# Attention and feed-forward on one core: the global units' probabilities turned on VectorE, one start flag per bank, single transfers for the last chunk

## The chip, the cores and the metric

The kernel runs on one core of a Trainium2 chip. The metric is the time of one execution in microseconds (us) on the device. The kernel before took 938.16 us in the median of three runs (934.59 to 939.67). An engine has its own instruction stream and runs it in order; engines wait for each other by semaphores. PE is TensorE's matmul, PEld its weight load, DVE VectorE, ACT ScalarE, POOL GpSimd, SP the engine that issues all transfers.

## The reference, cut to what matters

There are 8 batches, 8 heads of 64 columns, 32 global and 512 local tokens per batch. Global tokens attend to everything, local tokens to the global ones and to a window of 32 to each side. The result goes through a layer norm and a two-layer feed-forward with a residual.

```
k_all, v_all = cat(k_g, k_l), cat(v_g, v_l)
out_g = softmax(scale * q_g @ k_all.T) @ v_all                  # 32 rows per batch and head, 544 keys
s_ll  = where(|i - j| <= 32, scale * q_l @ k_l.T, -1e9)
out_l = softmax(cat(scale * q_l @ k_g.T, s_ll)) @ v_all         # 512 rows per batch and head
x     = cat(out_g, out_l)  as [batch, 576, 512]
xn    = (x - mean) / sqrt(var + 1e-6) * g_ln
out   = x + relu(xn @ w_ch1) @ w_ch2                            # 512 -> 2048 -> 512
```

## The kernel before, in words

**Feed-forward.** The 4096 local tokens are cut into eight chunks of 512 (chunk 0 to 7), the 256 global ones are the last chunk, chunk 8. A chunk runs over 16 slices `f` of the hidden layer. Each slice has 12 matmuls `ph` (L739, `hidden`), a relu `hh` on ACT (L750), the rounding rest `hl` on DVE (L754), and for each of its four token tiles 3 matmuls `acc` (L766, `out`). The matmuls of `out` for slice `f-1` stand behind `hidden` of slice `f`, so that `hl` has time. Every operand is split into a high and a low part, hence the factor 3.

**Attention beside it.** While TensorE works on chunk c, the attention of the next chunk is fed in between, in small steps. `step()` is called seven times in a slice (before each third of `hidden`, and before each of the four `out`); each call takes one `yield` from a queue `first`, or else one from the queue `side`. `put(place, run)` hangs a piece of attention on a place of the chunk; place `2f` is before `hidden(f)`, place `2f+1` behind it. The order on every engine is the order in which the program writes it.

A *pair* is two head pairs of a half batch: scores on PE (`sc`, L428), the row minimum and mask on DVE (L446), exponentials on ACT, 16 steps of two 32x32-block transposes on DVE (`pt`, L490), values on PE (`pv`, L500), and a scaled output on DVE (`x`, L519). A chunk has four pairs, at the places 1, 9, 17 and 25.

A *global unit* is one head pair of the global tokens of four batches. There are eight (two batch groups, four head pairs); chunks 1 to 6 hold one each, chunk 7 two. Its scores come in two passes of 272 keys (`sc`, L566), each read from its two PSUM banks by two DVE instructions (`gp`, L576). Then exponentials on ACT (L589), eight 128x128 transposes on PE into PSUM (`t`, L607), copied to SBUF on ACT (`gpt`, L609), the last 32 keys by DVE (L608). The values are 40 matmuls into one bank (`pv`, L620), two heads one after the other; the trace counts each twice. DVE scales them (`gx`, L634), SP stores them to a buffer `xs` in DRAM in four transfers (L642) and loads the next unit's inputs (`gq`, `gk`, `gv`, `gvt`).

**PSUM.** Scores, transposes and global values share a pool of two banks (tag `att`), `ph` and the pairs' `pv` share another pool of two. A matmul that wants a bank waits until its last reader is done.

**End of a chunk.** At slice 14 SP loads the residual rows `ob` from `xs` (L784); at the end DVE adds `acc` (L799) and SP stores the rows (L801). In chunk 8 a token tile's rows come from four batches, and `rows_global` cuts each tile into four transfers of 32 rows:

```
def rows_global(bg):
    return [(slice(i * SG, (i + 1) * SG), (bg * BG + i) * SA, SG) for i in range(BG)]
...
host(globals_[c - 1], (5, 12, 15, 21))     # chunks 1..6: scores 0, scores 1, transposes, values
host(globals_[c - 1], (1, 4, 8, 12))       # chunk 7, first unit
host(globals_[c], (16, 18, 21, 23))        # chunk 7, second unit
```

**Start.** GpSimd builds a band and from it four mask tiles in 22 copies (L153, L155) before the first scores are reduced.

Of the kernel before, what the change touches and what calls it, by code (L numbers as in the profile page):

```python
# [11 lines left out]
F32 = mybir.dt.float32  # L12
# [9 lines left out]
P = 128  # L22
WIN = 32
# [61 lines left out]
def attention_ffn_kernel(  # L85
# [59 lines left out]
    masks = {}  # L145
    for half in range(2):
        for qb in range(2):
            m = const.tile([P, P], F32, name=f"mask{half}{qb}")
            nc.gpsimd.memset(m, 0.0)
            for g in range(4):  # L150
                gp = slice(g * WIN, (g + 1) * WIN)
                at = 3 - (4 * qb + g) % 3
                nc.gpsimd.tensor_copy(m[gp, :at * WIN], band[gp, g * WIN:(g + at) * WIN])  # L153
                if at < 3:
                    nc.gpsimd.tensor_copy(  # L155
                        m[gp, (at + 1) * WIN:], band[gp, (g + at) * WIN:(g + 3) * WIN]
                    )
            if half == qb == 0:
                nc.gpsimd.memset(m[:WIN, :WIN], NEG / QSCALE)
# [113 lines left out]
    class Local:  # L273
# [105 lines left out]
        def output(self):  # L379
            hp = self.at[1]  # L380
            x = token_tile(0, hp)
# [13 lines left out]
    class Pair:  # L395
# [118 lines left out]
        def output(self):  # L514
            hp = self.at[1]
            x = token_tile(self.chunk, hp)
            nc.vector.reciprocal(self.ri, self.ri)
# [11 lines left out]
        def store(self):  # L529
            store_x(self.at[0], self.at[2], ready[self.chunk][-1])  # L530

        def norm(self):
            x = ready[self.chunk][-1]
            xn = ready[self.chunk][-1] = new_x()
            return Norm(x, range(2), xn)

    class Global:


        def __init__(self, bg, hp):  # L540
            self.at = bg, hp
            self.next = None

        def load(self):
# [11 lines left out]
        def scores(self, part):  # L556
# [31 lines left out]
            for h in range(2):  # L588
# [8 lines left out]
                yield  # L597

        def transposes(self):
            p = self.p  # L600
            pt = apool.tile([P, 2, SA], F32, name="gpt", tag="gk")
            self.pt = pt[:, :, :4 * P].rearrange("p h (c q) -> p h c q", c=4)
            self.tail = pt[:, :, 4 * P:]
            for h in range(2):
# [7 lines left out]
        def values(self):  # L612
            bg, hp = self.at
            pv = ps_a.tile([P, 512], F32, name="pv", tag="att")
            for h in range(2):
                hd = slice(h * D, (h + 1) * D)
                for c in range(5):
                    for i in range(BG):
                        ip = slice(i * SG, (i + 1) * SG)
                        nc.tensor.matmul(  # L620
                            pv[ip, hd],
                            self.pt[:, h, c, ip] if c < 4 else self.tail[ip, h, :],
                            self.v[c // 2][:, i, c % 2, hd] if c < 4 else self.vt[ip, hd],
                            start=(c == 0),
                            stop=(c == 4),
                            tile_position=(0 if c < 4 else i * SG, i * SG),
                            skip_group_check=True,
                        )
            ri = small.tile([P, 2], F32, name="gri", tag="ri2")
# [9 lines left out]
            )  # L639
            for i in range(BG):  # L640
                r0 = (bg * BG + i) * SA
                nc.sync.dma_start(  # L642
                    xs[r0:r0 + SG, hp * P:(hp + 1) * P], x[i * SG:(i + 1) * SG, :]
                )
            if self.next:
# [3 lines left out]
    def load_global_tokens(bg):  # L649
        x = ready[last_chunk][0]  # L650
        for i in range(BG):
            r0 = (bg * BG + i) * SA
            nc.sync.dma_start(x[i * SG:(i + 1) * SG, bg, :], xs[r0:r0 + SG, :])
        yield

    def rows_local(b, t):
        r0 = b * SA + SG + t * P
        return [(slice(0, P), r0, P)]

    def rows_global(bg):  # L660
        return [(slice(i * SG, (i + 1) * SG), (bg * BG + i) * SA, SG) for i in range(BG)]

# [55 lines left out]
    class Ffn:  # L718
# [52 lines left out]
        def run(self, f0, rows, stage, next_chunk):  # L771
            nt = self.nt
            obs = []
            for f in range(f0, NF):
# [4 lines left out]
                side.append(stage(f, 1))  # L779
                if f == NF - 2:  # L780
                    ob = fpool.tile([P, 4, DM], F32, name="ob", tag="ob")
                    for t in range(nt):
                        for ps, r0, nr in rows[t]:
                            nc.sync.dma_start(ob[ps, t, :], xs[r0:r0 + nr, :])  # L784
                        obs.append(ob[:, t, :])
# [8 lines left out]
            for t in range(nt):  # L794
# [4 lines left out]
                nc.vector.tensor_tensor(obs[t], self.acc[t], obs[t], op=ALU.add)  # L799
                for ps, r0, nr in rows[t]:  # L800
                    nc.sync.dma_start(out_flat[r0:r0 + nr, :], obs[t][ps])  # L801

# [27 lines left out]
    weights = [Weights(f) for f in range(NF)]  # L830
    ready = {}
    turned = []

    def token_tile(c, hp):
        got = ready.setdefault(c, [])
        if hp == 0:
            got.append(new_x())
        return got[-1]

    wcm, wtmp = open_pool("wtmp")  # L840
    acm, apool = open_pool("apool")

    def attend(u, before):

# [25 lines left out]
        while True:  # L870
# [7 lines left out]
            n += 1  # L878
            yield
        for _ in more:  # L880
            pass
# [5 lines left out]
    class First:  # L887
# [11 lines left out]
        def norm(self, h):  # L899
            x = ready[0][h]  # L900
            self.norms.append(Norm(x, range(2), new_x()))
            self.norms[h].stats()
# [15 lines left out]
        def does(self, token):  # L918
# [22 lines left out]
            elif op == "Nx":  # L941
                store_x(*chunks[0][n[0]], ready[0][n[0]])
            elif op == "Qx":
# [37 lines left out]
    for c, chunk in enumerate(chunks):  # L981
        if c == 1:
            globals_[0].load()
        if chunk is None:
            rows = [rows_global(bg) for bg in range(NBG)]
        else:
            rows = [rows_local(b, 2 * half + j) for b, half in chunk for j in range(2)]
# [10 lines left out]
        if 0 < c < last_chunk - 1:  # L998
            for f in PAIR_STEPS:
                u, before = new.pop(0)  # L1000
                put(2 * f + 1, lambda u=u, before=before: attend(u, before))
# [114 lines left out]
```

## Time and profile before

| | us |
|---|---|
| three runs, median | 938.16 (934.59 to 939.67) |
| profiled execution, its time | 938.44 |
| profiled execution, its span in the trace | 936.7 |
| PE busy | 911.1 (97%) |
| DVE busy | 572.0 (61%) |
| ACT busy | 313.4 (33%) |
| POOL busy | 36.2 (4%) |

The span is what the trace covers; the profiled execution took 1.7 us more. PE's busy time counts pipelined matmuls whose modelled ends overlap the next starts, so what a matmul costs is read from starts or from the chain of waits. That chain is followed back from the last instruction, at each step to what released it. The granted TensorE clock was 1.00 (2.4 GHz) in every window from 209 us on.

### The profile page before, as it was taken

What the parts mean: (1) busy time and instruction counts of PE and PEld (TensorE: products, weight loads), DVE (VectorE), ACT (ScalarE), POOL (GpSimd) and SP (SyncE); (2) the same over time, 40 slices, a digit from 0 to 9 for tenths busy, and PEclk for the clock granted to TensorE, in tenths of its full rate; (3) what the DMA queues carried; (4) which work ended last, traced back from release to release, by engine and by line L of the source; (5) the groups of instructions that cost most, each with busy time, mean ns of one, the idle gap of its engine ahead of it and who ended that gap; (6) DMA issues with size and microseconds to landing.
All of it is one profiled execution on the core that took longest, in us unless ns stands there. A gap on an engine that the chain in (4) does not pass through costs nothing.

```text
span 936.7 us, 21033 instructions
## 1 busy us (share of the span) xinstructions
PE 911.1 (97%) x8652; PEld 722.4 (77%) x8652; DVE 572.0 (61%) x1852; ACT 313.4 (33%) x839; POOL 36.2 (4%) x121
## 2 busy tenths in 40 slices
PE   5899999999999999999999999999999999999997
PEld 3677777777778778777878778777877777777896
DVE  4999958765786657765776657765776623111311
ACT  5888733331323323231323323231422312211210
POOL 3000000000000000000000000000000000000000
PEclk9799999999999999999999999999999999999999
DMA  9993245212633263212533263213533151031100
GB/s 349 419 415 118 87 136 194 101 58 89 228 121 98 76 214 117 84 51 103 214 121 97 76 233 99 89 53 119 190 121 98 46 170 57 1 102 60 51 18 23
DMA packets 48880, 119.33 MB, mean 127 GB/s; under 512 B 5008, under 2 KB 16272, under 8 KB 45712
## 3 DMA queue, kind: packets, MB, share of 16 engines
q1 hardware_dynamic: 48784, 117.98, 35.4%
q8 instruction: 68, 1.11, 0.5%
q14 instruction: 28, 0.23, 0.1%
HBM read 100.14 MB, written 17.83 MB: 126 GB/s over the span
## 4 chain that ended last, share of the span: by engine, by line
PE 90%; DVE 2%; ACT 1%; issue 0%; DVEq 0%
PE acc L766 40%; PE ph L739 40%; PE sc L428 3%; PE pv L500 3%; PE t L667 1%; PE pv L620 1%; PE sc L566 1%; PE t L607 1%; DVE pt L490 1%; DVE w L212 0%; DVE tmp L195 0%; DVE ob L799 0%; ACT tmp L183 0%; ACT w L208 0%; DVE hl L754 0%
## 5 line engine op out<-in xcount | busy, mean ns | idle before, releaser
L766 PE MATMUL acc<-w,hh 128*128 128x512 f32 x1088 | 342.1, 396 | 0.0
L739 PE MATMUL ph<-xh,w 128*128 128x512 f32 (+1 forms) x1240 | 310.6, 377 | 0.2 <-DVE x L519 0.2
L754 DVE SCALAR_TENSOR_TENSOR hl<-ph,hh 128x512 fp32r<-128x512 f32 (+1 forms) x147 | 95.6, 651 | 279.0 <-ACT hh L750 278.6
L739 PEld LDWEIGHTS ph<-xh,w 128*128 128x128 f32 x1240 | 219.3, 189 | 47.4 <-issue 1.2
L750 ACT ACTIVATE hh<-ph 128x512 fp32r<-128x512 f32 (+1 forms) x147 | 83.1, 565 | 496.4 <-PE ph L739 496.3
L766 PEld LDWEIGHTS acc<-w,hh 128*128 128x128 f32 x1088 | 205.7, 189 | 45.7
L490 DVE STREAM_TRANSPOSE pt<-p 32x128 f32<-32x128 f32 x768 | 232.2, 302 | 11.1
L766 PE MATMUL acc<-w,hl 128*128 128x512 f32 x544 | 222.6, 409 | 0.3 <-DVE hl L754 0.2
L739 PE MATMUL ph<-xl,w 128*128 128x512 f32 (+1 forms) x524 | 143.8, 396 | 0.8 <-DVE xl L688 0.8
L766 PEld LDWEIGHTS acc<-w,hl 128*128 128x128 f32 x544 | 102.5, 188 | 26.5 <-issue 3.0
L739 PEld LDWEIGHTS ph<-xl,w 128*128 128x128 f32 x524 | 96.2, 189 | 26.2 <-issue 3.5
L461 ACT ACTIVATE p<-p,mn 128x128 f32<-128x128 f32 x224 | 87.2, 391 | 33.5 <-DVE mn L446 31.5
L446 DVE CUSTOM_DVE_ANT_0 p<-sc,mask 128x128 f32<-128x128 f32 x224 | 51.1, 285 | 0.1
L461 ACT ACTIVATION_READ_ACCUMULATOR p<-p,mn 128x1 f32 x224 | 42.0, 188 | 0.0
L500 PE MATMUL pv<-v,pt 128*32 128x64 f32 x1792 | 32.1, 222 | 2.3 <-DVE pt L490 2.3
L500 PEld LDWEIGHTS pv<-v,pt 128*32 128x32 f32 x1792 | 27.0, 111 | 8.9 <-issue 6.2
L428 PE MATMUL sc<-e 64*32 64x128 f32 x1792 | 32.4, 274 | 0.0
L428 PEld LDWEIGHTS sc<-e 64*32 64x32 f32 x1792 | 24.9, 105 | 9.5 <-issue 9.1
L242 ACT ACTIVATE x<-x,rs 128x512 f32<-128x512 f32 x30 | 22.8, 809 | 20.6 <-DVE rs L236 20.6
L688 DVE SCALAR_TENSOR_TENSOR xl<-t,g_sb,xh 128x512 fp32r<-128x512 f32 (+1 forms) x36 | 24.6, 689 | 7.9 <-ACT xh L684 7.7
L684 ACT ACTIVATE xh<-t,g_sb 128x512 fp32r<-128x512 f32 (+1 forms) x40 | 24.9, 624 | 12.0 <-PE t L667 11.8
L519 DVE TENSOR_TENSOR x<-pv,ri 128x256 f32<-128x256 f32 x56 | 21.2, 420 | 8.3 <-PE pv L500 5.7
(73 smaller groups left out, 477.0 us busy)
## 6 DMA issues: line engine op xcount, KB each, us to landing
v<-in_eu SPq DMA_DIRECT2D x28, 1024.0 KB, 7.1
e<-in_eu SPq DMA_DIRECT2D x28, 672.0 KB, 5.3
raw<-in_wd SPq DMA_DIRECT2D x16, 1024.0 KB, 12.7
gk<-in_gk SPq DMA_DIRECT2D x8, 1088.0 KB, 5.2
xs<-x SPq DMA_DIRECT2D x32, 256.0 KB, 7.1
ob<-xs SPq DMA_DIRECT2D x32, 256.0 KB, 7.3
out<-ob SPq DMA_DIRECT2D x32, 256.0 KB, 2.1
gv<-in_gv SPq DMA_DIRECT2D x16, 512.0 KB, 6.8
```

The costliest lines, as they stand in the source:

```text
L242: nc.scalar.activation(self.xn[:, j, :], self.x[:, j, :], AF.Identity, bias=self.rs[:, 1, j:j + 1], scale=self.rs[:, 0, j:j + 1],)
L428: nc.tensor.matmul(sc[h][gp, at:at + P], self.e[hd, j, w * WIN:(w + 1) * WIN], self.e[hd, j, k0 * WIN:(k0 + 4) * WIN], start=True, stop=Tr ...
L446: nc.vector.tensor_tensor_reduce(out=self.p[:, j, c], in0=self.sc[h][:, at:at + P], in1=masks[self.at[2], qb], scale=-QSCALE, scalar=BIG, ...
L461: nc.scalar.activation(self.p[:, j, c], self.p[:, j, c], AF.Exp, bias=self.mn[:, j, c:c + 1], scale=-1.0, accum_out=self.sm[:, j, c:c + 1],)
L490: nc.vector.transpose(out=self.pt[rp, j, :, gp], in_=self.p[gp, j, :, rp])
L500: nc.tensor.matmul(self.pv[gp, at:at + D], self.pt[:, j, 2 * h + qb, gp], self.v[:, j, 4 * qb + g, h * D:(h + 1) * D], start=True, stop=Tr ...
L684: nc.scalar.activation(hi, t[:, :n], AF.Copy, scale=g_sb[:, kt:kt + 1])
L688: nc.vector.scalar_tensor_tensor(lo, t[:, :n], g_sb[:, kt:kt + 1], f32(hi), ALU.mult, ALU.subtract)
L739: nc.tensor.matmul(ph[:, :n], w[:, kt, :], xx[kt][:, part.start:part.start + n], start=(i == 0), stop=(i == 3 * KT - 1),)
L750: nc.scalar.activation(hh[:, :n], self.ph[f, start][:, :n], AF.Relu)
L754: nc.vector.scalar_tensor_tensor(hl[:, :n], self.ph[f, start][:, :n], 0.0, f32(hh[:, :n]), ALU.max, ALU.subtract)
L766: nc.tensor.matmul(self.acc[t], a[:, ts], w, start=(f == 0 and i == 0), stop=(f == NF - 1 and i == 2),)
```

## The change

Five edits, and an order that follows from them.

- The first seven global units no longer turn their probabilities on PE. `turns(h)` does it on DVE, in eight steps of two 32x32-block transposes for each head, straight from SBUF to SBUF. PE's eight transposes and ACT's two copies of these units are gone. The eighth unit (the second of chunk 7) keeps `transposes`.
- The places are others. `ride` hangs the scores on places 3 and 6 and the turns on 9 and 17; the values of chunks 1 to 6 are issued inside the last pair's `attend`, after four of its steps. In chunk 7 the turns are at 6 and 7 and the values behind them.
- `values` sets the start flag once in a bank, not once for each head, and takes the last 32 keys of both heads at the end.
- The masks of `half` 0 are copied by VectorE, those of `half` 1 by GpSimd as before.
- A global unit's store and the loads, residual rows and stores of chunk 8 are one transfer for each tile instead of four. For chunk 8 the tokens lie in a tile as (token, batch) instead of (batch, token), in every place alike. Token tiles are found by chunk and half instead of by the last one made.

```diff
     for half in range(2):
+        eng = nc.gpsimd if half else nc.vector
         for qb in range(2):
...
-                nc.gpsimd.tensor_copy(m[gp, :at * WIN], band[gp, g * WIN:(g + at) * WIN])
+                eng.tensor_copy(m[gp, :at * WIN], band[gp, g * WIN:(g + at) * WIN])
...
+        def turned(self):
+            if self.pt is None:
+                pt = apool.tile([P, 2, SA], F32, name="gpt", tag="gk")
+                self.pt = pt[:, :, :4 * P].rearrange("p h (c q) -> p h c q", c=4)
+                self.tail = pt[:, :, 4 * P:]
+
+        def turns(self, h):
+            self.turned()
+            p = self.p[:, h, :4 * P].rearrange("p (c q) -> p c q", c=4)
+            nc.vector.transpose(out=self.tail[:, h, :], in_=self.p[:, h, 4 * P:])
+            for n in range(8):
+                gp = slice(n // 2 * WIN, (n // 2 + 1) * WIN)
+                for r in range(n % 2 * 2, n % 2 * 2 + 2):
+                    rp = slice(r * WIN, (r + 1) * WIN)
+                    nc.vector.transpose(out=self.pt[rp, h, :, gp], in_=p[gp, :, rp])
+                yield
...
-            for h in range(2):
+            for h, c in [(h, c) for h in range(2) for c in range(4)] + [(0, 4), (1, 4)]:
...
-                            start=(c == 0),
+                        start=(h == c == 0),
...
-            for i in range(BG):
-                r0 = (bg * BG + i) * SA
-                nc.sync.dma_start(
-                    xs[r0:r0 + SG, hp * P:(hp + 1) * P], x[i * SG:(i + 1) * SG, :]
-                )
+            to = xs.rearrange("(b s) d -> b s d", b=B)[bg * BG:(bg + 1) * BG, :SG]
+            nc.sync.dma_start(to[:, :, hp * P:(hp + 1) * P], x)
...
+    def rows_global(a, bg):
+        return a.rearrange("(b s) d -> s b d", b=B)[:SG, bg * BG:(bg + 1) * BG, :]
...
-                for ps, r0, nr in rows[t]:
-                    nc.sync.dma_start(out_flat[r0:r0 + nr, :], obs[t][ps])
+                nc.sync.dma_start(rows[t](out_flat), obs[t])
...
+            if last and n == 4:
+                yield from last()
+                last = None
+        if last:
+            yield from last()
...
+        def ride(u, places):
+            for n, place in enumerate(places[:2]):
+                put(place, lambda n=n: first.append(u.scores(n)) or ())
+            for n, place in enumerate(places[2:]):
+                put(place, lambda n=n: u.turns(n))
...
-            host(globals_[c - 1], (5, 12, 15, 21))
+                last = globals_[c - 1].values if f == PAIR_STEPS[-1] else None
+                put(2 * f + 1, lambda u=u, before=before, last=last: attend(u, before, last))
+            ride(globals_[c - 1], (3, 6, 9, 17))
...
-            host(globals_[c - 1], (1, 4, 8, 12))
+            ride(globals_[c - 1], (1, 4, 6, 7))
+            put(7, globals_[c - 1].values)
```

The lines of the changed kernel have other numbers: `hidden` is L751, `out` L778, the global scores L569 with their reads L579, the tail transposes L611, the turns L616, `hl` L766, the stores L811.

First, TensorE in chunk 2, at the first pass of the global scores. `sc<-gk,gq` is a pass of scores, `ph` and `acc` are the feed-forward. Before:

```order
L739 MATMUL ph<-xh_3098,w 128x512 x2
L739 MATMUL ph<-xh_3120,w 128x512 x2
L566 MATMUL sc<-gk,gq 32x272 x8
L739 MATMUL ph<-xl_3099,w 128x512 x2
L739 MATMUL ph<-xl_3121,w 128x512 x2
L739 MATMUL ph<-xh_3098,w 128x512 x2
L739 MATMUL ph<-xh_3120,w 128x512 x2
L766 MATMUL acc_3300<-w,hl 128x512
```

Now:

```order
L751 MATMUL ph<-xh_3111,w 128x512 x2
L751 MATMUL ph<-xh_3133,w 128x512 x2
L569 MATMUL sc<-gk,gq 32x272 x8
L751 MATMUL ph<-xl_3112,w 128x512 x2
L751 MATMUL ph<-xl_3134,w 128x512 x2
L569 MATMUL sc<-gk,gq 32x272 x8
L751 MATMUL ph<-xh_3111,w 128x512 x2
L751 MATMUL ph<-xh_3133,w 128x512 x2
```

The second pass stood four slices later, behind another pair; now it stands one step, four `ph` matmuls, behind the first, as it does in all of the chunks 1 to 6. The first pass has kept its place.

Second, VectorE in chunk 7, from the second pass's reads to the unit's output `gx`. `gpt<-gp` are the block transposes, 128x32 the last 32 keys. Before:

```order
L576 TENSOR_SCALAR gp,gmn<-sc,gmn 128x272 x2
L754 SCALAR_TENSOR_TENSOR hl<-ph,hh 128x512 x2
L608 STREAM_TRANSPOSE gpt<-gp 128x32 x2
L754 SCALAR_TENSOR_TENSOR hl<-ph,hh 128x512 x2
L632 RECIPROCAL gri<-gri 128x2
L634 TENSOR_TENSOR gx<-pv,gri 128x128
```

Now:

```order
L611 STREAM_TRANSPOSE gpt<-gp 128x32
L616 STREAM_TRANSPOSE gpt<-gp 32x4x32 x6
L766 SCALAR_TENSOR_TENSOR hl<-ph,hh 128x512
L616 STREAM_TRANSPOSE gpt<-gp 32x4x32 x10
L611 STREAM_TRANSPOSE gpt<-gp 128x32
L616 STREAM_TRANSPOSE gpt<-gp 32x4x32 x4
L766 SCALAR_TENSOR_TENSOR hl<-ph,hh 128x512
L616 STREAM_TRANSPOSE gpt<-gp 32x4x32 x12
L766 SCALAR_TENSOR_TENSOR hl<-ph,hh 128x512
L649 RECIPROCAL gri<-gri 128x2
L651 TENSOR_TENSOR gx<-pv,gri 128x128
```

VectorE has 32 more transposes for the unit, 12 of them behind the `hl` that comes before the values. On TensorE the values stand four `out` tiles and two thirds of a `hidden` behind the `hidden` of that `hl`.

Third, the end of SP's stream, from the last global unit's store on. `out<-ob` are the stores of the result. Before:

```order
L642 DMA xs<-gx 32x128 x4
L653 DMA x<-xs 32x512 x4
L784 DMA ob<-xs 128x512 x4
L801 DMA out<-ob 128x512 x4
L784 DMA ob<-xs 32x512 x8
L801 DMA out<-ob 32x512 x8
```

Now:

```order
L658 DMA xs<-gx 4x32x128
L665 DMA x<-xs 128x1x512
L795 DMA ob<-xs 128x512 x4
L811 DMA out<-ob 128x512 x4
L795 DMA ob<-xs 128x1x512 x2
L811 DMA out<-ob 32x4x512 x2
```

The eight last stores have become two, of 256 KB each.

## Rows read from the trace of the kernel before

**Rows 1.** The page: busy us of each engine, share of the span, instructions

```profile
PE 911.1 (97%) x8652; PEld 722.4 (77%) x8652; DVE 572.0 (61%) x1852; ACT 313.4 (33%) x839; POOL 36.2 (4%) x121
```

**Rows 2.** The chain of waits from 200 us to the end, by line

```profile
by line: PE acc L766 44.0%; PE ph L739 43.4%; PE sc L428 3.1%; PE pv L500 3.1%; PE pv L620 1.8%; PE t L667 1.6%; PE sc L566 1.3%; PE t L607 0.9%; DVE ob L799 0.1%; issue 0.0%
```

**Rows 3.** The same chain from 198 to 212 us: start, length, what

```profile
204.61 0.44 PE t L607 x4
205.05 0.93 PE ph L739 x4
```

**Rows 4.** Groups by line: count, busy us, mean ns, idle before

```profile
L607 PE MATMUL t<-ident,gp 128*128 128x128 f32 x64 | 9.6, 272 | 0.0
...
L750 ACT ACTIVATE hh<-ph 128x512 fp32r<-128x512 f32 (+1 forms) x147 | 83.1, 565 | 496.4 <-PE ph L739 496.3
```

**Rows 5.** Busy time in a stretch of 103 us: PE, PEld, DVE, ACT, POOL

```profile
313.00:416.00 103.00, 103.00 (x1022) 81.21 (x1021) 70.83 (x250) 30.64 (x93) 3.04 (x9) 1.00 0.35 123
```

**Rows 6.** Timeline of chunk 2, PE and DVE: start, length, instruction

```profile
277.22 2.52 DVE L490 STREAM_TRANSPOSE pt<-p 32x128 f32<-32x128 f32 x8
...
278.62 0.69 PE L566 MATMUL sc<-gk,gq 64*32 64x272 f32 x16
...
279.24 1.20 PE L739 MATMUL ph<-xl,w 128*128 128x512 f32 x4
279.78 0.44 DVE L576 TENSOR_SCALAR_CACHE_REDUCE gp<-sc 128x272 f32<-128x272 f32 x1
...
280.14 0.43 DVE L576 TENSOR_SCALAR_CACHE_REDUCE gp<-sc 128x272 f32<-128x272 f32 x1
280.28 1.09 PE L739 MATMUL ph<-xh,w 128*128 128x512 f32 x4
```

**Rows 7.** Timeline of chunk 1, a pair's last transposes and its values

```profile
156.41 0.69 DVE L754 SCALAR_TENSOR_TENSOR hl<-ph,hh 128x512 fp32r<-128x512 f32 x1
...
157.13 3.82 DVE L490 STREAM_TRANSPOSE pt<-p 32x128 f32<-32x128 f32 x12
...
161.01 1.06 PE L500 MATMUL pv<-v,pt 128*32 128x64 f32 x26 [0.99 <-DVE pt L490]
```

**Rows 8.** Timeline of chunk 1, a global unit's values on PE

```profile
225.47 0.65 PE L620 MATMUL pv<-gv,gpt 128*32 128x64 f32 x32
...
226.05 0.31 PE L620 MATMUL pv<-gvt,gpt 32*32 32x64 f32 x8
...
226.30 0.65 PE L620 MATMUL pv<-gv,gpt 128*32 128x64 f32 x32
```

**Rows 9.** Timeline of the end: DVE's last adds, SP's last stores

```profile
930.10 1.39 DVE L799 TENSOR_TENSOR ob<-acc,ob 128x512 f32<-128x512 f32 x2 [1.26 <-PE acc L766]
...
930.81 3.60 SPq L801 DMA_DIRECT2D out<-ob  x8
```

**Rows 10.** Transfers: KB each, median us from issue to landing

```profile
ob<-xs SPq DMA_DIRECT2D x32, 256.0 KB, 7.3
out<-ob SPq DMA_DIRECT2D x32, 256.0 KB, 2.1
...
out<-ob SPq DMA_DIRECT2D x8, 64.0 KB, 1.7
```

**Rows 11.** Timeline of the start: the band on POOL, the first reduction

```profile
2.32 0.34 POOL L136 TENSOR_SCALAR_AFFINE_SELECT band<-band 128x192 f32<-128x192 f32 x1
...
5.86 0.29 DVE L321 CUSTOM_DVE_ANT_0 p<-sc,mask 128x128 f32<-128x128 f32 x1 [5.86 <-PE sc L304]
```

**Rows 12.** Timeline of chunk 1's end: SP's residual loads, adds, hl, hidden

```profile
238.93 2.22 SPq L784 DMA_DIRECT2D ob<-xs  x4
...
259.36 2.80 DVE L799 TENSOR_TENSOR ob<-acc,ob 128x512 f32<-128x512 f32 x4
...
264.90 0.69 DVE L754 SCALAR_TENSOR_TENSOR hl<-ph,hh 128x512 fp32r<-128x512 f32 x1 [2.74 <-ACT hh L750]
...
266.28 1.20 PE L739 MATMUL ph<-xh,w 128*128 128x512 f32 x4
```

More of the change, by code (lines that the diff above doesn't have):

```diff
@@ L380, in output @@
             hp = self.at[1]
-            x = token_tile(0, hp)
+            x = token_tile(0, self.at[2])
             nc.vector.reciprocal(self.ri, self.ri)
@@ L515, in output @@
             hp = self.at[1]
-            x = token_tile(self.chunk, hp)
+            x = token_tile(self.chunk, self.at[2])
             nc.vector.reciprocal(self.ri, self.ri)
@@ L529, in store @@
         def store(self):
-            store_x(self.at[0], self.at[2], ready[self.chunk][-1])
+            b, _, half = self.at
+            store_x(b, half, token_tile(self.chunk, half))
         def norm(self):
-            x = ready[self.chunk][-1]
-            xn = ready[self.chunk][-1] = new_x()
-            return Norm(x, range(2), xn)
+            half = self.at[2]
+            xn = ready.setdefault(self.chunk, [None, None])[half] = new_x()
+            return Norm(token_tile(self.chunk, half), range(2), xn)
     class Global:
@@ L542, in __init__ @@
             self.next = None
+            self.pt = None
         def load(self):
@@ L597, in scores @@
                 yield
+        def turned(self):
[13 more added lines that the diff above has]
+                yield
         def transposes(self):
             p = self.p
-            pt = apool.tile([P, 2, SA], F32, name="gpt", tag="gk")
-            self.pt = pt[:, :, :4 * P].rearrange("p h (c q) -> p h c q", c=4)
-            self.tail = pt[:, :, 4 * P:]
+            self.turned()
             for h in range(2):
@@ L614, in values @@
             pv = ps_a.tile([P, 512], F32, name="pv", tag="att")
-            for h in range(2):
+            for h, c in [(h, c) for h in range(2) for c in range(4)] + [(0, 4), (1, 4)]:
                 hd = slice(h * D, (h + 1) * D)
-                for c in range(5):
-                    for i in range(BG):
[L619 to L623, printed above, removed]
-                            start=(c == 0),
-                            stop=(c == 4),
-                            tile_position=(0 if c < 4 else i * SG, i * SG),
-                            skip_group_check=True,
-                        )
+                for i in range(BG):
+                    ip = slice(i * SG, (i + 1) * SG)
+                    nc.tensor.matmul(
+                        pv[ip, hd],
+                        self.pt[:, h, c, ip] if c < 4 else self.tail[ip, h, :],
+                        self.v[c // 2][:, i, c % 2, hd] if c < 4 else self.vt[ip, hd],
+                        start=(h == c == 0),
+                        stop=(c == 4),
+                        tile_position=(0 if c < 4 else i * SG, i * SG),
+                        skip_group_check=True,
+                    )
             ri = small.tile([P, 2], F32, name="gri", tag="ri2")
@@ L650, in load_global_tokens, with rows_local @@
         x = ready[last_chunk][0]
-        for i in range(BG):
-            r0 = (bg * BG + i) * SA
-            nc.sync.dma_start(x[i * SG:(i + 1) * SG, bg, :], xs[r0:r0 + SG, :])
+        nc.sync.dma_start(x[:, bg, :], rows_global(xs, bg))
         yield
-    def rows_local(b, t):
+    def rows_local(a, b, t):
         r0 = b * SA + SG + t * P
-        return [(slice(0, P), r0, P)]
-    def rows_global(bg):
-        return [(slice(i * SG, (i + 1) * SG), (bg * BG + i) * SA, SG) for i in range(BG)]
+        return a[r0:r0 + P, :]
+    def rows_global(a, bg):
+        return a.rearrange("(b s) d -> s b d", b=B)[:SG, bg * BG:(bg + 1) * BG, :]
     def turn_tokens(xn, kt, out, bank):
@@ L830, in attention_ffn_kernel, with token_tile, attend @@
     weights = [Weights(f) for f in range(NF)]
-    ready = {}
+    ready, tokens = {}, {}
     turned = []
[L834 to L838, printed above, removed]
+    def token_tile(c, half):
+        if (c, half) not in tokens:
+            tokens[c, half] = new_x()
+        return tokens[c, half]
     wcm, wtmp = open_pool("wtmp")
     acm, apool = open_pool("apool")
-    def attend(u, before):
+    def attend(u, before, last):
         if u:
@@ L899, in norm @@
         def norm(self, h):
-            x = ready[0][h]
+            x = token_tile(0, h)
             self.norms.append(Norm(x, range(2), new_x()))
@@ L941, in does @@
             elif op == "Nx":
-                store_x(*chunks[0][n[0]], ready[0][n[0]])
+                store_x(*chunks[0][n[0]], token_tile(0, n[0]))
             elif op == "Qx":
@@ L984, in attention_ffn_kernel @@
         if chunk is None:
-            rows = [rows_global(bg) for bg in range(NBG)]
+            rows = [lambda a, bg=bg: rows_global(a, bg) for bg in range(NBG)]
         else:
-            rows = [rows_local(b, 2 * half + j) for b, half in chunk for j in range(2)]
+            rows = [
+                lambda a, b=b, t=2 * half + j: rows_local(a, b, t)
+                for b, half in chunk for j in range(2)
+            ]
         at = {}
```

12 lines of the change are left out of this document (4 added, 8 removed).

## The prediction

> **What bounds the kernel.** The page's busy shares come first: PE is busy for 97% of the span, VectorE for 61% [rows 1]. A share of pipelined matmuls proves little, so the chain of waits is read next. From 200 us on it holds nothing but PE: the named lines of PE add up to 99.4%, and VectorE stands in it with 0.1% [rows 2]. So behind the start every microsecond that PE is spared comes off the end, and work given to VectorE costs only where PE comes to wait for it. The transposes that leave PE are 0.9% of that chain.
>
> Third come the windows: in 103 us of the middle, about the length of a chunk, VectorE is busy for 70.83 us and ACT for 30.64 [rows 5]. VectorE has about 32 us a chunk to give away. Last comes the timeline of the few places where the new order puts an instruction close behind something it needs.
>
> **The change part by part.** Sums are made against the profiled execution, 938.44 us with a span of 936.7; the median of the runs is 0.28 us lower. A change of less than 0.5%, 4.7 us, can't be told from none here.
>
> *Transposes off PE.* A group of four is 0.44 us of the chain [rows 3], the same in the group that follows it. Seven units have two groups each: 14 x 0.44 = 6.2 us saved. The share over all 16 groups gives the other end: 0.9% of 736.7 us is 6.6, or 0.41 a group, 5.8 in all. I take 6.2.
>
> Each of these transposes is shown as 272 ns long [rows 4], which is more than twice what it takes in the chain, since neighbours overlap. The Trainium skill, page "TensorE: Matmul & The Clock Gate", section "Part 4: PE-mode transpose", gives about 275 ns for one in a kernel. As a duration this trace agrees with 272; as a price the chain says 0.11, and the measurement decides. Counted by the page's figure the 56 transposes would be worth 15.4 us, an estimate.
>
> *Turns on VectorE.* A unit gets 32 turns. Eight of a pair's turns, of the same shape, take 2.52 us [rows 6], 0.315 each, so a unit costs VectorE 10.1 us and seven cost 71 us. The 32 us that are free in a chunk hide it on the average. In time: a slice has seven steps, so at most 14 turns (4.4 us) and one `hl` (0.7 us [rows 12]), 5.1 us against 24 matmuls on PE. Four of these take 0.93 us [rows 3], so a slice takes 5.6. VectorE keeps up even where every step has a turn. ACT loses 14 copies, which nothing waited for. I count 0; bounds follow with the rivals.
>
> The Trainium skill, page "VectorE: DVE Perf Modes", section "Rules for kernel authors", speaks against this edit: it sends a 128x128 transpose to TensorE where PSUM will do. For the engine's own work that agrees with the trace (16 turns of 0.315 us for what PE does in 0.88), but the trace has PE as the bound, so VectorE's time isn't the price.
>
> *Second pass of the scores.* In chunks 2 to 6 it now stands one step behind the first, and both use the two banks of the pool `att`, so it waits until VectorE has read the first pass out of both. In chunk 2 the first pass starts on PE at 278.62, but VectorE is still in eight turns until 279.74 and reads the second bank until 280.14 + 0.43 = 280.57 [rows 6]. These rows stand in the same order in the changed kernel. PE would be ready at 280.28, after the four matmuls between. A hand-over from VectorE to PE takes 0.06 (160.95 to 161.01 [rows 7]), so PE waits until 280.63, 0.35 us. In chunks 3 to 6 VectorE starts the read at the same distance from the scores. In chunk 1 it is free earlier, and I count nothing. Five times 0.35 is 1.8 us lost. The lower end is 0. The upper end is VectorE 1 us later (the longest single wait of PE for turns is 0.99 [rows 7]): 5 x 1.35 = 6.8. I take 1.8, from the nearest row.
>
> *Values of chunk 7.* They stand right behind the last turns. The model is chunk 1 before, where 12 turns behind an `hl` end 4.54 us after that `hl` began, and PE waits [rows 7]. In chunk 7 there are 12 turns as well. An `hl` begins about 0.9 us after its `hidden` (a relu of 0.57 [rows 4] and two hand-overs, an estimate), so the turns end at 5.4. PE gets there after 12 `acc` and 8 `ph` at 0.234, 4.7 us, has about 0.3 us of the first head to do, and waits 0.4 us. Bounds: 0, and 1 for a wait like the 0.99. In chunks 1 to 6 the values come long behind the turns: no wait.
>
> *One start flag and the tails together.* Nothing is left out. Eight tail entries take 0.25 us (226.05 to 226.30 [rows 8]), 31 ns each, and 32 others 0.58 (225.47 to 226.05), 18 each. If the 0.1 us excess is the switch between the two tile shapes, a unit switches once less: 8 x 0.1 = 0.8 gained; if it belongs to the tails, 0. A loss has no cause, since operands, count and bank are the same. I take 0.4 gained.
>
> *Single transfers.* At the end VectorE's last add is done at 930.10 + 1.39 = 931.49, but SP needs 3.60 us for the eight stores [rows 9], 0.45 each, so the last starts at 930.81 + 7 x 0.45 = 933.96. Now SP is free at 931.3, and the second of two stores starts at 931.5, 2.5 us earlier. A 256 KB store lands 2.1 us after its issue, one of 64 KB 1.7 [rows 10]: 0.4 later. Gain: 2.1 us. The bounds are 2.5 (it lands like the small one) and a loss of 3.1 (it lands after 7.3 us like the residual loads [rows 10], 931.5 + 7.3 against 933.96 + 1.7). I take 2.1, because that row is the same line and size, and nothing else is in the queue by then. The other merged transfers spare SP time that no engine waits for.
>
> *Masks.* VectorE's 14 instructions begin when the band is ready at 2.66 and must be done by 5.86, when the first reduction starts [rows 11]: 0.23 us for each. At that reduction's 0.29 they would end at 6.7, 0.9 late; but it handles 128 partitions and 128 columns, they 32 and at most 96. I take 0, range 0 to 0.9. GpSimd ends earlier, which nothing waits for.
>
> **Sum.** -6.2 + 1.8 + 0.4 - 0.4 - 2.1 = -6.5 us: 938.44 becomes 931.9. I predict 932 us.
>
> **The rivals.**
>
> *The waits eat the gain.* VectorE is 1 us further behind at the second score passes, through the turns that now stretch over the end of the chunk before. For it: it has less slack everywhere. Against it: at the start of chunk 2 VectorE idles 2.74 us for `hh` [rows 12], which absorbs four late turns (1.3 us). Time: 938.44 - 6.2 + 6.8 + 0.4 - 0.4 - 2.1 = 936.9, no change.
>
> *The residual rows come late: slower.* The next unit's loads (2.2 MB) now stand on SP in front of `ob`. They are issued only after the values, so `ob` is issued some 13 us later than the 238.93 of before, its last tile at about 253.5 (counted in steps from the new order), while the adds start at 259.36 [rows 12] plus the 1.7 us of values that this stretch now holds, 261.0. At 7.3 us to land the last tile is there at 260.8, in time. At twice that it lands at 268.1; the add (0.7) and the `hl` behind it (0.7) end at 269.5, while PE wants the bank of that `hl` at 266.28 + 1.7 = 268.0 [rows 12]: 1.5 us of wait in each of six chunks, 9 us, 941 us in all. From a landing of about 14 us on it decides the sign (6.5 / 6 = 1.1 us of wait). For it: a load of this size takes 7.3 us where a store in a quiet queue takes 2.1 [rows 10], so traffic ahead counts, and more of it stands ahead now. Against it: that 7.3 holds other traffic already, and it would have to double.
>
> *The transposes are worth their shown length.* 56 x 0.272 = 15.2 instead of 6.2: 922.9 us. Against it stands the chain [rows 3]; for it, little but that the chain shares out overlapping work by a rule. By the figure of the Trainium skill's "Part 4: PE-mode transpose" (page "TensorE: Matmul & The Clock Gate") the time would be 922.7, an estimate.
>
> **How the numbers follow.** Forecast 0.62, waits 0.25, slower 0.08, full length 0.05. The forecast's own range is 928 to 936: its low end has 0.8 for the tails, 2.5 for the end and no waits (938.44 - 6.2 - 0.8 - 2.5 = 928.9) less a little for the spread of the runs; its high end has the wait terms half way to their bounds. Over all cases 927 to 938.5 leaves out the slower case, the full-length case and a tail of the waits. Faster by over 0.5% means under 933.5: about three quarters of the forecast's share, a little of the waits, and all of the full-length case, 0.55. Slower means over 942.9: 0.07. The rest, 0.38, is no change.
>
> **What would show it.** In the new profile: no PE group of `t<-ident,gp` beyond 8 entries and 56 fewer matmuls; PE's waits for `gp` five times at some 0.35 us and one for the turns near 0.4; VectorE some 71 us busier, with `hl` still mostly waiting for `hh`; two last stores, the second issued when the last add ends; values near 1.6 us a unit. It is wrong if PE waits for `hl`, `ob` or the turns in each chunk, if the end still lies over 4 us behind the last add, or if PE's chain shows other lines grown by what the transposes left.

## The result: 0.9% faster, and the profile after

The changed kernel took 929.44 us in the median of six runs (927.59 to 930.43), the kernel before 938.27 beside it (934.59 to 939.67). The ratio is 0.9908, with a 95% interval of 0.9889 to 0.9928. Two more sets of runs gave 0.9911 (0.9897 to 0.9925) and 0.9913 (0.9898 to 0.9927). The profiled execution took 929.66 us, its span 927.9. The forecast was 932.

Page of the changed kernel, busy us of each engine (against [rows 1]):

```profile
PE 904.3 (97%) x8596; PEld 716.3 (77%) x8596; DVE 640.1 (69%) x2090; ACT 304.8 (33%) x825; POOL 33.5 (4%) x107
...
L616 DVE STREAM_TRANSPOSE gpt<-gp 32x128 f32<-32x128 f32 x224 | 67.2, 300 | 3.2
```

PE has 56 instructions fewer, VectorE 68.1 us more, nearly all of it in the 224 turns. The chain of waits from 200 us on, by line (against [rows 2]):

```profile
by line: PE acc L778 43.8%; PE ph L751 43.6%; PE sc L429 3.1%; PE pv L501 3.1%; PE t L679 1.6%; PE pv L637 1.5%; PE sc L569 1.3%; PE t L625 0.1%; DVE ob L810 0.1%; issue 0.0%
```

It is PE's chain still. The unit's transposes shrank from 0.9% to 0.1% (the eighth unit's eight), the values from 1.8% to 1.5%. No line of VectorE came into it but the last add.

**Where the time went.** The profiled executions differ most before the first group of twelve `acc` at about 90 us: in the eleven whose chain shows this mark it lay anywhere from 87.7 to 90.5 us, with no regard to the edit. Behind the mark each stretch of the changed kernel repeats to 0.1 us, apart from one clock effect told at the end. So parts are compared behind it. Pieces of the chain at that mark and at the ends of chunks 1 and 2, before (start, length, what):

```profile
89.63 3.06 PE acc L766 x12
...
257.92 3.51 PE acc L766 x15
363.02 3.51 PE acc L766 x15
```

and after, with the ends of chunks 6 and 7:

```profile
89.34 3.07 PE acc L778 x12
...
256.54 3.50 PE acc L778 x15
360.77 3.50 PE acc L778 x15
...
776.54 3.50 PE acc L778 x15
874.85 3.51 PE acc L778 x15
```

From the mark to the end of the span before took 936.7 - 89.63 = 847.07 us, after 927.9 - 89.34 = 838.56: 8.5 us less. Two more traces of the changed kernel give 838.63 and 838.58; of the kernel before there is one trace. A chunk with one unit (363.02 - 257.92) went from 105.10 to 104.23.

**Second pass of the scores.** PEld's waits from 200 us on (total us, times, longest), then the chain in chunk 2, then the timeline there (the first pass, the read of its second bank, the second pass):

```profile
PEld sc L569 <- issue: 3.3, 9, 0.4
...
PEld sc L569 <- DVE gp L579: 1.8, 5, 0.4
```

```profile
277.31 0.62 PE sc L569 x16
...
279.05 0.86 PE sc L569 x14
```

```profile
277.24 0.69 PE L569 MATMUL sc<-gk,gq 64*32 64x272 f32 x16
...
278.73 0.43 DVE L579 TENSOR_SCALAR_CACHE_REDUCE gp<-sc 128x272 f32<-128x272 f32 x1
...
278.98 0.93 PE L569 MATMUL sc<-gk,gq 64*32 64x272 f32 x16
```

The second row's five waits with 1.8 us together are what the prediction said. But the second pass is only 0.24 us longer than the first (0.86 to 0.62). The first row shows that 0.36 is no wait by itself: ahead of the other passes, which wait for nothing, PEld has 3.3 / 9 = 0.37 us of idle time as well. PE's real wait lies inside the pass: it begins at 278.98, but VectorE reads the second bank until 279.16.

**Values.** PE's timeline in chunk 1 (against [rows 8]), and the chain's pieces of a unit's values in chunk 1 and of chunk 7's first unit:

```profile
238.80 1.10 PE L637 MATMUL pv<-gv,gpt 128*32 128x64 f32 x64
239.83 0.43 PE L637 MATMUL pv<-gvt,gpt 32*32 32x64 f32 x16
```

```profile
238.87 1.39 PE pv L637 x80
...
808.76 1.59 PE pv L637 x80
```

A unit took 0.58 + 0.25 + 0.58 + 0.25 = 1.66 before [rows 8]; now 1.39. In chunk 7 it is 1.59, so the wait for the turns costs 0.20.

**End.** Timeline of the last adds and stores (against [rows 9]), the residual loads of the whole kernel, and the stores issued from 920 us on (against [rows 10]):

```profile
923.14 1.39 DVE L810 TENSOR_TENSOR ob<-acc,ob 128x512 f32<-128x512 f32 x2 [1.26 <-PE acc L778]
...
923.86 1.29 SPq L811 DMA_DIRECT2D out<-ob  x2
```

```profile
ob<-xs SPq DMA_DIRECT2D x34, 256.0 KB, 6.7
```

```profile
out<-ob SPq DMA_DIRECT2D x2, 256.0 KB, 2.4
```

The span ends 927.9 - 924.53 = 3.4 us behind the last add; before it was 936.7 - 931.49 = 5.2. The two last stores land 2.4 us after their issue.

**Residual rows and `hl`.** SP's issue of chunk 1's residual loads, VectorE's first add there (against [rows 12]), and VectorE's longest sum of waits:

```profile
248.84 2.12 SPq L795 DMA_DIRECT2D ob<-xs  x4
```

```profile
258.74 0.69 DVE L810 TENSOR_TENSOR ob<-acc,ob 128x512 f32<-128x512 f32 x1
```

```profile
DVE hl L766 <- ACT hh L762: 201.9, 111, 5.5
```

The loads are issued 9.9 us later than before, where some 13 were foreseen. The last lands at about 250.96 + 6.7 = 257.7 (an estimate from the median), before the adds, which wait for no transfer. `hl` still waits for `hh`, and among PEld's waits from 200 us on there is none for `hl`.

### The profile page after: what moved, and what is told of

It reads as the page before. It is cut to its first block, busy times and chain, and to the rows that moved or that the text cites. A ratio compares the mean times of both kernels' runs of the same rounds, so it can differ in the third digit from the quotient of the medians.

```text
span 927.9 us, 21081 instructions
## 1 busy us (share of the span) xinstructions
PE 904.3 (97%) x8596; PEld 716.3 (77%) x8596; DVE 640.1 (69%) x2090; ACT 304.8 (33%) x825; POOL 33.5 (4%) x107
## 4 chain that ended last, share of the span: by engine, by line
PE 90%; DVE 2%; ACT 1%; issue 0%; DVEq 0%
PE ph L751 40%; PE acc L778 40%; PE sc L429 3%; PE pv L501 3%; PE t L679 1%; PE pv L637 1%; PE sc L569 1%; DVE pt L491 1%; DVE w L213 0%; DVE tmp L196 0%; DVE ob L810 0%; ACT tmp L184 0%; ACT w L209 0%; DVE hl L766 0%; PE tp L477 0%
## 5 line engine op out<-in xcount | busy, mean ns | idle before, releaser
L778 PE MATMUL acc<-w,hh 128*128 128x512 f32 x1088 | 342.2, 396 | 0.0
L751 PE MATMUL ph<-xh,w 128*128 128x512 f32 (+1 forms) x1240 | 311.3, 378 | 0.2 <-DVE x L520 0.2
L751 PEld LDWEIGHTS ph<-xh,w 128*128 128x128 f32 x1240 | 218.9, 189 | 50.2 <-issue 3.4
L766 DVE SCALAR_TENSOR_TENSOR hl<-ph,hh 128x512 fp32r<-128x512 f32 (+1 forms) x147 | 95.7, 651 | 213.9 <-ACT hh L762 213.6
L778 PEld LDWEIGHTS acc<-w,hh 128*128 128x128 f32 x1088 | 205.4, 189 | 46.0
L778 PE MATMUL acc<-w,hl 128*128 128x512 f32 x544 | 221.7, 408 | 0.3 <-DVE hl L766 0.2
L751 PE MATMUL ph<-xl,w 128*128 128x512 f32 (+1 forms) x524 | 142.6, 393 | 0.8 <-DVE xl L700 0.8
L778 PEld LDWEIGHTS acc<-w,hl 128*128 128x128 f32 x544 | 102.4, 188 | 24.4 <-DVE hl L766 0.6
L751 PEld LDWEIGHTS ph<-xl,w 128*128 128x128 f32 x524 | 97.2, 189 | 27.3 <-issue 3.9
L616 DVE STREAM_TRANSPOSE gpt<-gp 32x128 f32<-32x128 f32 x224 | 67.2, 300 | 3.2
```

What stands on the lines that cost most here:

```text
L616: nc.vector.transpose(out=self.pt[rp, h, :, gp], in_=p[gp, :, rp])
L751: nc.tensor.matmul(ph[:, :n], w[:, kt, :], xx[kt][:, part.start:part.start + n], start=(i == 0), stop=(i == 3 * KT - 1),)
L766: nc.vector.scalar_tensor_tensor(hl[:, :n], self.ph[f, start][:, :n], 0.0, f32(hh[:, :n]), ALU.max, ALU.subtract)
L778: nc.tensor.matmul(self.acc[t], a[:, ts], w, start=(f == 0 and i == 0), stop=(f == NF - 1 and i == 2),)
```

## The experiments

Each is the changed kernel with the edit shown. Times are compared as ratios to the kernel before on the same chip. The changed kernel has 0.9911 (0.9897 to 0.9925) beside three of them: the transposes, the old order and the later score pass. Beside the masks and the last of the better kernels it has 0.9913. The other four ran on a chip where only the kernel before ran beside them; they are set against 0.9911, or compared behind the mark.

**The transposes back on PE.** Seven units use `transposes` again.

```diff
-            for n, place in enumerate(places[2:]):
-                put(place, lambda n=n: u.turns(n))
+            put(places[-1], lambda: first.append(u.transposes()) or ())
...
-            put(7, globals_[c - 1].values)
+            put(9, globals_[c - 1].values)
```

> The first seven global units are turned on PE again (eight transposes and two copies each), at the later of the two places the turns have now; the values of chunk 7's first unit stand one slice later; all else as in the changed kernel. Theory, the chain's price of 0.44 us a group of four: 14 groups, +6.2, less the 0.4 us wait in chunk 7 that goes: +5.8 us against the changed kernel. Rival, the length shown of each (272 ns): 56 x 0.272 = +15.2. Rival, transposes hidden by the loads beside them: 0. VectorE's busy time falls by about 70 us; that alone is worth nothing by the theory.

It took 934.61 us, ratio 0.9972 (0.9961 to 0.9984). From the mark to the end it is 844.36 us (932.4 - 88.04), 5.8 more than the changed kernel. Its chain in chunk 5, and two ends of chunks:

```profile
643.46 0.44 PE t L625 x4
...
644.82 0.44 PE t L625 x4
```

```profile
256.06 3.51 PE acc L778 x15
361.17 3.50 PE acc L778 x15
```

A chunk takes 105.10 instead of 104.23: 0.87 for two groups, 0.435 each. The chain's price holds, the shown length (+15.2) falls. VectorE is 67.1 us less busy (573.0) and that gives nothing. The Trainium skill, page "VectorE: DVE Perf Modes", section "Rules for kernel authors", sends a 128x128 transpose to TensorE where PSUM will do as its destination. Doing so costs this kernel 5.8 us, because PE is the bound.

**The old order of the values, with one start flag.**

```diff
-            for h, c in [(h, c) for h in range(2) for c in range(4)] + [(0, 4), (1, 4)]:
+            for h, c in [(h, c) for h in range(2) for c in range(5)]:
```

> The values of a global unit in the order of before (head 0 with its tail, then head 1 with its tail), but with the one start flag of the changed kernel. The values of a unit take 1.39 us in the changed kernel and 1.66 before. Theory, the order (two switches between the tile shapes 128x32 and 32x32 fewer): 1.66 us a unit again, +2.2 us for eight units against the changed kernel. Rival, the flag: 1.39 a unit, 0. Rival, the price of the prediction (0.05 a unit): +0.4.

It took 932.12 us, ratio 0.9942 (0.9929 to 0.9955). PE's timeline in chunk 1:

```profile
237.79 0.65 PE L637 MATMUL pv<-gv,gpt 128*32 128x64 f32 x32
238.37 0.31 PE L637 MATMUL pv<-gvt,gpt 32*32 32x64 f32 x8
238.62 0.65 PE L637 MATMUL pv<-gv,gpt 128*32 128x64 f32 x32
239.20 0.31 PE L637 MATMUL pv<-gvt,gpt 32*32 32x64 f32 x8
239.45 1.20 PE L751 MATMUL ph<-xh,w 128*128 128x512 f32 x4
```

1.66 us again, to the hundredth the value of before [rows 8], though the flag is the new one. So the flag is worth nothing and the order all of it. A chunk takes 104.49, 0.25 longer (360.27 - 255.78 in its chain); from the mark on the kernel takes 840.38 (928.7 - 88.32), 1.8 more. It is below the 2.2 because the first unit of chunk 7 takes 1.66 too, with no wait for the turns in it, where the changed kernel's takes 1.59 with one.

**More changes between the two tile shapes.** Each 32x32 tail stands behind one of the eight groups of 128x32.

```diff
-            for h, c in [(h, c) for h in range(2) for c in range(4)] + [(0, 4), (1, 4)]:
+            seq = []
+            for h in range(2):
+                for c in range(4):
+                    seq += [(h, c, range(BG)), (h, 4, [c])]
+            for h, c, part in seq:
...
-                for i in range(BG):
+                for i in part:
...
-                        stop=(c == 4),
+                        stop=(c == 4 if i == 3 else c == 3),
```

> The same 40 matmuls of a global unit's values, with one start flag, but each of the eight 32x32 tails stands behind one of the eight 128x32 groups: 15 changes of tile shape inside a unit in place of 1. Theory, each change costs about 0.125 us (0.25 us a unit went with two changes): 14 more by 8 units by 0.125, +14 us, a unit's values 3.1 us long. Rival, the cost is not the change of shape but the two heads' turn about or the place of the tails as such: +2 us or less, 1.4 to 1.66 us a unit.

It took 953.12 us, ratio 1.0161 (1.0148 to 1.0175): +23.7 us. The chain in chunk 3, then windows there (PE, PEld, DVE, ACT, POOL busy, granted clock, DMA share, GB/s):

```profile
453.80 3.79 PE pv L641 x80
```

```profile
453.00:456.00 3.00, 3.00 (x54) 1.76 (x52) 0.96 (x4) 0.00 (x0) 0.83 (x3) 1.00 1.00 326
456.00:459.00 3.00, 3.00 (x36) 2.08 (x36) 0.00 (x0) 0.00 (x0) 0.00 (x0) 0.80 0.28 106
459.00:462.00 3.00, 3.00 (x10) 2.32 (x10) 1.73 (x6) 0.60 (x1) 0.00 (x0) 0.63 0.00 0
```

The mechanism holds and the size was low: 14 more changes cost 2.40 us a unit, 0.17 each, where two fewer gave 0.27, 0.135 each. Eight units make 19.2. In chunks 1, 3 and 7 the granted clock fell behind the values, though PE was busy throughout (in chunk 1 its mean was 0.83 from 240 to 250 us). Chunk 3 took 108.14 where its neighbours took 106.64: 1.5 more. Three times that and the 19.2 make 23.7. Whether the price is that of the change itself, or of short runs that can't overlap their like, these two runs don't tell apart.

**The second score pass a step later.**

```diff
-            ride(globals_[c - 1], (3, 6, 9, 17))
+            ride(globals_[c - 1], (3, 7, 9, 17))
```

> In chunks 1 to 6 the second score pass stands at place 7 instead of 6, a few steps later. Theory: PE's five waits of 0.35 us for the reads of the first pass go, -1.8 us, and nothing new is waited for. Rival: the wait only moves, to the next user of the two banks or to the turns; 0. Rival: the 0.35 shown is no cost in the chain, since loads and matmuls overlap; 0 with the waits gone.

It took 927.88 us, ratio 0.9897 (0.9884 to 0.9909); from the mark on 837.43 (926.3 - 88.87), 1.1 less. Chain in chunk 2:

```profile
276.81 0.62 PE sc L569 x16
...
280.20 0.62 PE sc L569 x16
```

The waits are gone and both passes take 0.62, but a chunk gets only 0.22 us shorter (104.01, 360.06 - 256.05 in its chain), not 0.35. PEld's idle time ahead of the passes adds up to 5.1 us as before (3.3 and 1.8); it is only put down to no wait any more:

```profile
PEld sc L569 <- issue: 5.1, 14, 0.4
```

Fourteen of 0.36 us instead of nine and five: a pass has this gap in any case, so the row says nothing of the price. The first theory is right in kind, but 0.35 was foreseen and 0.22 came.

**Four transfers for each tile of chunk 8 again.**

```diff
-                nc.sync.dma_start(rows[t](out_flat), obs[t])
+                for i, r in enumerate(rs):
+                    nc.sync.dma_start(r, obs[t][i * m:(i + 1) * m])
```

(and its loads and residual rows likewise)

> In chunk 8 the loads, the residual rows and the stores are four transfers for each tile again; the global units' own stores stay single. Theory: all of the price lies behind VectorE's last add, where 3.4 us become some 5.2 again; +1.9 us against the changed kernel. Rival: the last stores overlap each other whatever their number; 0. Rival: the single transfers also help the loads ahead of them; more than +1.9, with part of it before the last add.

It took 931.42 us, ratio 0.9933 (0.9917 to 0.9948). Its last adds and stores:

```profile
922.12 1.39 DVE L816 TENSOR_TENSOR ob<-acc,ob 128x512 f32<-128x512 f32 x2 [1.26 <-PE acc L779]
```

```profile
922.84 3.60 SPq L822 DMA_DIRECT2D out<-ob  x8
```

The span of 928.7 ends 5.2 us behind the last add at 923.51, against 3.4. From chunk 7's end to the last add both kernels take 49.68 us, and chunk 7, in which chunk 8's tokens are loaded, takes 98.35 against 98.31. So chunk 8's other merged transfers bring nothing. The global units' own stores stayed single here, so they are not tested.

**Every turn done twice.**

```diff
-                    nc.vector.transpose(out=self.pt[rp, h, :, gp], in_=p[gp, :, rp])
+                    for _ in range(2):
+                        nc.vector.transpose(out=self.pt[rp, h, :, gp], in_=p[gp, :, rp])
```

> Every block transpose of the turns of the first seven global units is done twice, which gives VectorE some 71 us more and nothing else. Theory, cover with an edge: four turns a step (1.26 us) in place of two no longer fit into a step of 0.8 us, so within a slice VectorE falls 3.9 us behind; its rounding rest has about 2.4 us before PE wants its bank; so PE waits about 1.5 us for each of 14 heads and some 5 us for the values in chunk 7: +10 to +30, say +25 us. Rival, all hidden (VectorE is still under 80% busy): 0. Rival, VectorE's time is the price: +71.

It took 972.89 us, ratio 1.0377 (1.0363 to 1.0391): +43.5 us for 67.9 us more of VectorE (708.0). PEld's waits from 200 us on, and a window in chunk 2 behind a wait of 3.06 us for `hl` (columns as above):

```profile
PEld ph L752 <- DVE hl L767: 22.3, 11, 4.4
PEld pv L638 <- DVE gpt L617: 12.0, 5, 3.2
```

```profile
350.00:355.00 5.00, 4.92 (x88) 3.66 (x88) 4.86 (x28) 3.30 (x16) 0.74 (x2) 0.66 0.31 111
```

None of the three numbers came true. The cover has an edge, as the first theory says, and PE comes to wait for the bank of `hl` as it says. But it took each head alone. In truth the second head's turns stand right behind the pair's, VectorE is behind since the first head (busy for over 4.5 us of each 5 us from 320 to 350), and the backlog adds up to waits of 3 us and more: 34.3 us in these two rows, which leave 9.2 of the 43.5. Behind such a wait the clock was granted at 0.66 in the mean of five microseconds, and it falls in each of the chunks 1 to 7, where the changed kernel has 1.00 from 200 us on. How much of the 9.2 that explains was not measured.

**The masks back on GpSimd.**

```diff
-        eng = nc.gpsimd if half else nc.vector
+        eng = nc.gpsimd
```

> All mask copies on GpSimd again, as before. Theory, the masks were no part of the gain: 0 against the changed kernel, and the first reduction again at 5.9 us. Rival: the copies shared between two engines start the first chunk earlier; up to +0.5 without them.

It took 928.21 us, ratio 0.9896 (0.9880 to 0.9911), where the changed kernel beside it had 0.9913 (0.9898 to 0.9927): no difference can be told. The first reduction, in this kernel and in the changed one:

```profile
6.00 0.29 DVE L322 CUSTOM_DVE_ANT_0 p<-sc,mask 128x128 f32<-128x128 f32 x1 [6.00 <-POOL mask L156]
```

```profile
5.87 0.29 DVE L322 CUSTOM_DVE_ANT_0 p<-sc,mask 128x128 f32<-128x128 f32 x1 [0.71 <-PE sc L305]
```

0.13 us at the start, and 838.53 (926.4 - 87.87) behind the mark against 838.56. (The trace of the kernel before has 26 copies of the masks, 16 of L153 and 10 of L155, not 22.)

**Towards a better one.** First the eighth unit on VectorE too, with the later second pass.

```diff
+            ride(globals_[c - 1], (3, 7, 9, 17))
...
-            put(7, globals_[c - 1].values)
-            host(globals_[c], (16, 18, 21, 23))
+            put(9, globals_[c - 1].values)
+            ride(globals_[c], (16, 18, 19, 20))
+            put(23, globals_[c].values)
```

> The second score pass a step later, as in the run before it; the eighth unit is turned on VectorE too; the values of chunk 7's first unit stand one slice later. Theory: -1.1 for the five second passes (0.22 a chunk, as that run showed), -0.9 for two groups of transposes, -0.2 for the wait for the turns in chunk 7; -2.2 us against the changed kernel, about 927.2. Rival: in chunk 7, with two units, VectorE falls behind and PE waits for the turns or the rounding rest; the gain of 1.1 is gone, 928 to 930.

It took 928.27 us, ratio 0.9898 (0.9884 to 0.9911): no better than the later pass alone. The rival held. The values of the eighth unit stand right behind its last turns and wait:

```profile
849.72 0.63 PE L637 MATMUL pv<-gv,gpt 128*32 128x64 f32 x26 [0.56 <-DVE gpt L616]
```

They take 2.24 us (848.40 to 850.64) instead of 1.39, and that 0.85 is about all that the two groups of transposes gave. The first unit's values didn't move at all: `side` is a queue, in which they stood behind 16 steps of turns at place 9 as at place 7. So the first unit's values had to stand later and the eighth unit's turns earlier (the edit is against the run just told):

```diff
-            put(9, globals_[c - 1].values)
-            ride(globals_[c], (16, 18, 19, 20))
+            put(11, globals_[c - 1].values)
+            ride(globals_[c], (15, 17, 18, 19))
```

> The second score pass a step later in chunks 1 to 6; the eighth unit is turned on VectorE too, all of it a place earlier than in the last such run, so that the values stand two steps behind its turns; the values of chunk 7's first unit stand one step later. Theory: -1.1 (five second passes), -0.9 (two groups of transposes), -0.2 (the wait of chunk 7's values for the turns): -2.2 us against the changed kernel, 927.2, and both units' values in chunk 7 take 1.39. Rival: the values wait for the turns again, as in the last such run (2.25 instead of 1.39), and 0.9 of it is gone; 928.1.

It took 926.11 us (925.37 to 927.82), ratio 0.9872 (0.9855 to 0.9888), where the changed kernel beside it had 930.42 and 0.9913 (0.9898 to 0.9927). It beats both kernels. Its chain at the values of chunk 7, and at the ends of chunks 6 and 7:

```profile
807.73 1.39 PE pv L637 x80
...
844.55 1.39 PE pv L637 x80
```

```profile
774.58 3.50 PE acc L778 x15
871.77 3.51 PE acc L778 x15
```

Both units take 1.39, chunk 7 97.19 us instead of 98.31: 1.1, which is 0.9 and 0.2. Behind the mark it is 836.17 (924.8 - 88.63), 2.4 less than the changed kernel; the rest of the difference between the medians is no larger than the spread of the start.

The changed kernel itself ran along twice as the measure.

> The changed kernel once more, as the measure for the other runs of this call. Every theory: 929.4 us, 0.991 of the kernel before.

> The changed kernel once more, as the measure for the other two runs of this call. Every theory: 929.4 us, 0.991 of the kernel before.

It took 929.36 us and 930.42.

## Why the prediction was right

The forecast of 932.0 lay 2.6 above the median, inside its own range and with the right sign. Its mechanism held: PE is the chain, the transposes are worth their price in it, and VectorE hides the turns. By its terms:

| term | predicted | measured |
|---|---|---|
| transposes off PE | -6.2 | -6.1 (14 x 0.435, put back) |
| turns on VectorE | 0 | 0 |
| second score pass | +1.8 | +1.1 (taken away) |
| values of chunk 7 | +0.4 | +0.2 (1.59 against 1.39) |
| start flag and tails | -0.4 | -2.0 (chunks of the old order) |
| single transfers | -2.1 | -1.8 (3.4 against 5.2) |
| masks | 0 | 0 |
| sum | -6.5 | -8.6; the trace has -8.5 behind the mark |

- *Transposes.* The step that read 0.44 from the chain and not 272 ns from the row of one instruction decides most of the result. The Trainium skill's duration (page "TensorE: Matmul & The Clock Gate", section "Part 4: PE-mode transpose"), about 275 ns, is the row's, and no price: put back, a transpose costs 0.11 us.
- *Turns.* Hidden, by the count of 5.1 us in a slice of 5.6. The doubled run shows how close that count stands to the edge: the second dose cost 0.64 us for each us of VectorE. (Where the prediction sets 16 turns against 0.88 us of PE, a unit's 32 belong; nothing in the sum hangs on it.)
- *Second pass.* Five waits came, for the read that was foreseen, but PE loses 0.22 to 0.24 in each and not 0.35. The step that failed is small: PE's arrival was taken from the start of the next `ph`, 1.66 us behind the first pass (280.28 - 278.62), but the second pass begins 1.74 behind it (278.98 - 277.24), so less waiting is left. That PEld's row shows 0.36 is chance, since passes without a wait show it too.
- *Values of chunk 7.* The wait came at half its size. The prediction gave PE about 0.3 us of the first head to do; by [rows 8] a head's 32 entries take 0.58.
- *Start flag and tails.* This is the term that was mis-sized. The prediction saw 0.1 us of excess in a unit's eight tail entries and counted one change of shape fewer, at half a chance. By the order the unit has two fewer: into the first head's tails, and back out of them. Each is worth 0.135, also on the side of the 128x32 group that follows. 8 x 0.27 against 8 x 0.05 is most of what the forecast missed. The 2.0 us lie outside the bounds that the term was given (0 to 0.8). The low end of the range held all the same, because it counted no waits and 1.3 us of them came; so far it was luck. The Trainium skill, page "TensorEngine Tiling (Array Packing)", section "Key Properties", says that a change of the tiling mode, not of the tile alone, drains TensorE. The two runs agree in so far as each change costs time, 0.135 to 0.17 us; a drain as such they don't show.
- *Single transfers.* The last stores landed after 2.4 us, where 2.1 was taken: 1.8 and not 2.1.
- *Rivals.* The waits did not eat the gain: the row has five of 0.35, none of 1.35. The residual rows land some 1 us before the adds; the slower case would have needed twice the 6.7 us that came. The shown length of the transposes is no price.

## What to carry to other kernels

Where PE is the whole chain, an instruction's price on it is what its group adds to the chain, not the duration in its row; a group that is put back alone measures it in one run. A wait listed for the weight loads is no price either: 0.36 us were listed here, and 0.22 came back when it went. Work moved to an engine with idle time is free up to an edge, and the edge lies in the stretch where its jobs stand back to back, not in its busy share: put a few steps between the moved work and whoever waits for it. Small matmuls of one tile shape belong together.

## What the runs showed of the hardware

- Going between tiles of 128x32 and 32x32 cost PE about 0.135 us (two changes fewer) to 0.17 us (14 more) each time, with the same matmuls.
- The granted clock fell behind idle time of PE, and behind 3.79 us of small tiles whose shape changed again and again (in three of the eight places). This makes a wait dearer than its length. In chunk 1 PE waited 0.29, 0.98 and 0.99 us for a pair's turns; there twelve of the thirteen traces show a drop, and the run with four transfers, with waits of 0.28, 0.98 and 0.99, does not. The window behind those waits in the changed kernel, and in the run with four transfers:

```profile
161.00:163.00 2.00, 2.00 (x25) 1.55 (x14) 1.60 (x11) 1.65 (x8) 0.00 (x0) 0.50 1.11 372
```

```profile
161.00:163.00 2.00, 1.82 (x31) 1.52 (x32) 1.77 (x12) 1.34 (x7) 0.00 (x0) 1.00 1.07 365
```

  0.50 is the lower level, 1.2 GHz. From the mark to the end of chunk 1 the first takes 167.20 us and the second 165.68 (255.49 - 89.81): 1.5 us for one drop. Why that one run was spared stays open.
